# When the halves of the sine tiles are compared: beside the cosine's, or behind the cosine's five rows of tiles

## The chip, the core and the metric

The kernel runs on one NeuronCore of a Trainium2 chip. The metric is device time in microseconds. Five engines have instruction streams of their own, in order: TensorE (PE in the profile; its weight loads PEld), VectorE (DVE), ScalarE (ACT), GpSimd (POOL) and SyncE (SP). The last two issue the transfers from HBM here; SP's queue is in order, so a load that waits for its buffer holds every load behind it. A line number like L387 is a line of the kernel.

## What is computed

```python
h  = x + (Cr @ (xn @ Dr.T) - Ci @ (xn @ Di.T))   # xn = layernorm(x); x is 2048 x 576
r  = layernorm(h) @ w_r                          # one score per token
t  = argmax(r)                                   # a single token
y  = (silu(xs @ w_gate) * (xs @ w_up)) @ w_down  # xs: its normalized row; 4608 hidden columns
out = h + layernorm(h),  and y * sigmoid(r[t]) added to row t
```

`Cr`, `Ci` (2048 x 2048) and `Dr`, `Di` (576 x 576) are the cosine and sine matrices of a Fourier transform, given as inputs in float32.

## The kernel before

**Using and checking the symmetry.** The four matrices are inputs, so the kernel may not assume what is in them. It computes the transform with folded operands (the cosine and sine of an angle give those of its mirror images) and, beside it, compares the parts of the matrices that it uses with those that it doesn't. Each compare writes differences as bfloat16 into a buffer `Q`, ScalarE squares and sums a part of `Q` into one column of `DS`, and at the end a sum over the threshold sends the program into a general path that is not taken here. So all of the matrices is loaded, though only a part of it is multiplied.

**Tiles of the sequence matrices.** A tile (j, i) holds 9 x 128 columns on 128 partitions, 576 KB; i is 0 for the cosine and 1 for the sine. Group one is the rows j = 1 to 5, group two 6, 7, 0 and 8. The tiles that PE multiplies lie in slots of `D`: five slots D0 for the cosine of group one, five D1 for its sine, four D2 (later the cosine of group two). Seven slots `R` and freed slots of `D` form a ring through which all others pass: the mirrored part of a tile (a gather that POOL issues, L301) and the tile of the mirror row 16 - j (SP, L357).

**The checks.** `c_check(j, i)` makes three compares on VectorE: `off_s` for j, `off_s` for 16 - j (L375 each, 896 columns) and `off_t` between the two tiles (L380, 1152 columns). They fill one of the two parts of `Q`, and one square follows (L368, 2944 columns). A ring slot is free for its next load when its last compare has run. There are five checks for the cosine of group one and five for its sine; "check 3" below is that of row 3. `off_h` compares the left half of a tile with the mirrored right half (L387), two instructions for one or two tiles; these are called *halves* here. They read tiles that stay in place for PE, and free no ring slot. In `c_half` the halves of a cosine pair and of the sine pair of the same rows go into one part of `Q`, with one square for both (2304 columns; 1152 for the single fifth row).

**PE's work.** `seq` multiplies the folded tokens by the tiles of a group, in five steps of which 0, 1 and 4 need the cosine tiles and 4, 2 and 3 the sine tiles; `keep` brings each result into a block of `Z` (ScalarE L579, then VectorE L583, called *Z block* here); `hid` multiplies `Z` by the hidden matrices (L610). Then VectorE adds the residual (L619), scores the tokens, picks one, and the weights of its feed-forward part stream through the same buffers (SP L1173), with products on VectorE and POOL and the last product on PE (L1228).

**What sets the order.** The kernel holds a planner: every step is entered with `add`, an estimated duration and what it depends on; `Plan.order` lays out all engines in time, taking on each engine, of the steps that are ready, the one with the longest way to the end, and the instructions are then written out in that order. A buffer is assigned when a step is entered, so the order of the calls from L948 to L999 sets which slot of the ring and which part of `Q` a check gets (`qs.take`, two parts in turn), and with the part which square it waits for:

```python
    for c, m in HALVES[0]:
        c_half(0, c, m)
    for j in GROUPS[0][:3]:
        c_check(j, 0)
    w_first()
    for j in GROUPS[0][3:]:
        c_check(j, 0)
    for n in (0, 1, 4, 2, 3):
        seq_step(0, n)
        keep_step(0, n)
```

Of the kernel before, what the change touches and what calls it, by code (L numbers as in the profile page):

```python
# [14 lines left out]
P = 128  # L15
# [22 lines left out]
GROUPS = [[1, 2, 3, 4, 5], [6, 7, 0, 8]]  # L38
# [5 lines left out]
HALVES = [[(0, 2), (2, 2), (4, 1)], [(0, 2), (2, 2)]]  # L44
# [8 lines left out]
HM = P // 2  # L53
# [17 lines left out]
class Plan:  # L71
# [6 lines left out]
    def add(self, eng, dur, fn, *deps, tail=0.0, push=0.0):  # L78
        flat = []
        for d in deps:  # L80
            flat += d if isinstance(d, list) else [d]
        n = {"eng": eng, "dur": dur, "fn": fn, "deps": [d for d in flat if d], "tail": tail, "push": push}
        n["i"] = len(self.ops)
        self.ops.append(n)
        return n
# [57 lines left out]
def kernel(  # L143
# [172 lines left out]
    Q = QT.bitcast(BF16).rearrange("p (n w) -> p n w", n=2)  # L316
# [62 lines left out]
        o = Q[:, u % 2, 14 * P : QW].rearrange("p (k m) -> p k m", m=P)  # L379
        dve.tensor_tensor(o, C[NK - j, i, False], C[j, i, False][:, :, ::-1], op=SIGN[i])  # L380

    def off_h(g, c, n, i, u):

        o = Q[:, u % 2, i * 9 * n * HM : (i + 1) * 9 * n * HM].rearrange("p (c k m) -> p c k m", k=9, m=HM)
        t = DT[g, i][:, c : c + n]
        for k, op in enumerate((OP.subtract, OP.add)):
            dve.tensor_tensor(o[:, :, k::2, :], t[:, :, k::2, 0:HM], t[:, :, k::2, HM:P], op=op)  # L387
# [296 lines left out]
    add = plan.add  # L684

    def then(f, *args):
        return lambda: f(*args)
# [25 lines left out]
    for k, n in X_LOADS:  # L713
        d = in_turn("SP" if k < 9 else "POOL", then(load_x, k, n), 0.295 * n)
# [11 lines left out]
    for a, b in X_RUNS:  # L726
# [4 lines left out]
        m = [add("ACT", 0.95, then(measure, k), f, push=push) for k, f in zip(ks, r)]  # L731
# [70 lines left out]
    CU = {}  # L802
# [11 lines left out]
            LAST["SP"], d = load("SP", then(load_c, None, j, i, False), 0.59, w, LAST["SP"])  # L814
            CU[j, i, False] = u, d

    def c_half(g, c, m):
        u, w = qs.take()
        cus = [[CU[j, i, False] for j in GROUPS[g][c : c + m]] for i in range(2)]
        n = [  # L820
            add("DVE", 0.16 + 0.62 * m, then(off_h, g, c, m, i, u), [d for _, d in cus[i]], w)
            for i in range(2)
        ]
        for i in range(2):
            for b, _ in cus[i]:
                users[b].append(n[i])
        squares(u, 9 * m * P, n)

    def squares(u, w, n, ps=P):
        SQUARES.append(add("ACT", 0.3 + w / 1200, then(square, u, w, ps), n))  # L830
        qs.users[u].append(SQUARES[-1])

    def c_check(j, i):

        u, w = qs.take()
        u0, d0 = CU[j, i, False]
        c_load(j, i, True)
        u1, d1 = CU[j, i, True]
        n = [add("DVE", 1.08, then(off_s, j, i, u, 0), d0, d1, w)]
        users[u0] += n  # L840
        users[u1] += n
        free.append(u1)
        if j in PAIRS:
            m = NK - j
            c_load(m, i, False)
            c_load(m, i, True)
            (u2, d2), (u3, d3) = CU[m, i, False], CU[m, i, True]
            n.append(add("DVE", 1.08, then(off_s, m, i, u, 1), d2, d3, w))
            users[u3].append(n[1])
            n.append(add("DVE", 1.36, then(off_t, j, i, u), d0, d2, w))  # L850
            users[u0].append(n[2])
            users[u2] += n[1:]
            free.extend([u3, u2])
        if u0[0] == "D1":
            free.append(u0)
        squares(u, QW if j in PAIRS else 7 * P, n)
# [94 lines left out]
        for b in [b for b in free if type(b) is tuple and b[0] == tag]:  # L951
            free.remove(b)

    for c, m in HALVES[0]:
        c_half(0, c, m)
    for j in GROUPS[0][:3]:
        c_check(j, 0)
    w_first()
    for j in GROUPS[0][3:]:
        c_check(j, 0)  # L960
    for n in (0, 1, 4, 2, 3):
        seq_step(0, n)
        keep_step(0, n)
# [18 lines left out]
    for i in range(2):  # L982
        for j in GROUPS[1]:
            c_check(j, i)
    for c, m in HALVES[1]:
        c_half(1, c, m)
    for c in range(2):
        hid_step(0, c)
    for n in (0, 1):
# [514 lines left out]
```

## Time and profile before

| | |
|---|---|
| time, median of 3 runs | 200.77 us (200.58 to 201.01) |
| the profiled execution | 201.27 us, span 199.2 us |
| VectorE busy | 166.1 us (83%), 419 instructions |
| ScalarE busy | 140.5 us (71%), 259 instructions |
| TensorE busy | 130.4 us (65%) |
| GpSimd busy | 122.8 us (62%) |
| moved by DMA | 77.81 MB, 391 GB/s over the span |

A busy row reads: engine, busy time, share of the span, number of instructions. The rows in tenths cut the span into 40 slices of 5 us. A row of a window gives, after its length, the busy time and number of instructions of PE, PEld, DVE, ACT and POOL, the granted clock, the mean busy share of the 16 DMA engines, and GB/s. A row of waits reads: engine, line, what ended the wait, us in total, times, longest. A row in order of time gives the start, the time to the end of the last of its instructions, engine, line, operation, tiles and count, and in brackets the idle time before it and what ended that. "SPq" is SP's queue; the duration of its rows is that of the issue, not of the transfer. Where the releaser named in a wait had long been done, the wait was for something else, often a transfer.

### The profile page before, as it was taken

To read this page: it belongs to the slowest core of one execution; us is meant where nothing else is said; L and a number is where in the kernel's file an instruction comes from. 1 tells how busy PE (TensorE), PEld (TensorE's weight loads), DVE (VectorE), ACT (ScalarE), POOL (GpSimd) and SP (SyncE) were. 2 spreads that over 40 slices of the span, in tenths; PEclk is the share of its full clock that TensorE was granted. 3 is DMA by queue.
4 is the path that set the end of the run, shared out by engine and by line. 5 is a ranking of instruction groups with operands and counts; after the bars stand their busy time and mean duration, and the time that the engine had idled before them with its cause. 6 is when DMAs were issued, how large, how long until landed. Compare 5 with 4: busy or idle time off the path is not lost. (4 is left out here: it accounts for less than half of the span.)

```text
span 199.2 us, 2787 instructions
## 1 busy us (share of the span) xinstructions
PE 130.4 (65%) x758; PEld 89.9 (45%) x758; DVE 166.1 (83%) x419; ACT 140.5 (71%) x259; POOL 122.8 (62%) x134
## 2 busy tenths in 40 slices
PE   0007989999999989899999996600241444085840
PEld 0005667764767778677877774400121111043220
DVE  4389997989999859997999999999839997899410
ACT  2298863783987794799587599997629999786400
POOL 6578888495528878998870000006439999998500
PEclk9999999999999999999999999985555555555798
DMA  5999999999979999999999999999999999999991
GB/s 190 361 418 415 411 411 409 409 372 346 402 275 366 415 398 391 404 407 412 407 401 418 420 420 422 427 414 423 422 428 425 428 422 420 431 420 412 422 387 42
DMA packets 14491, 77.81 MB, mean 391 GB/s; under 512 B 1855, under 2 KB 1859, under 8 KB 11143
## 3 DMA queue, kind: packets, MB, share of 16 engines
q1 hardware_dynamic: 10463, 56.56, 70.8%
q0 software_dynamic: 4000, 21.03, 26.3%
q8 instruction: 7, 0.11, 0.2%
q14 instruction: 13, 0.11, 0.1%
q10 hardware_dynamic: 8, 0.00, 0.0%
HBM read 72.86 MB, written 6.49 MB: 398 GB/s over the span
## 5 line engine op out<-in xcount | busy, mean ns | idle before, releaser
L368 ACT ACTIVATE Q<-Q 128x2944 bf16<-128x2944 bf16 (+5 forms) x26 | 55.4, 2133 | 19.9 <-DVE Q L375 7.0
L610 PE MATMUL py<-W,Z 128*128 128x289 f32 x180 | 45.3, 408 | 2.3 <-DVE X L619 2.3
L565 PE MATMUL ps<-D,XF 128*128 128x320 f32 (+3 forms) x216 | 45.0, 408 | 1.2 <-DMA D<-in_ct_dram 0.8
L301 POOL DMA_INDIRECT R<-in_ct_dram,ic x21 | 34.1, 1625 | 14.5 <-DVE Q L375 10.5
L610 PEld LDWEIGHTS py<-W,Z 128*128 128x128 f32 x180 | 33.7, 189 | 13.6 <-issue 2.9
L565 PEld LDWEIGHTS ps<-D,XF 128*128 128x128 f32 (+1 forms) x216 | 32.1, 172 | 13.8 <-issue 2.5
L1201 POOL TENSOR_TENSOR D<-D,Z 128x1152 f32<-128x1152 f32 x8 | 20.8, 2618 | 1.2 <-SPq L1331 1.2
L667 POOL DMA_DIRECT2D out_dram<-X x1 | 0.6, 606 | 30.0 <-ACT X L661 30.0
L301 POOL DMA_INDIRECT D<-in_ct_dram,ic x11 | 16.1, 1468 | 3.4 <-issue 2.4
L498 ACT ACTIVATE junk<-X,XT 128x576 bf16<-128x576 f32 x16 | 12.4, 772 | 8.0 <-DVE W L459 6.5
L1206 ACT ACTIVATE junk<-D 128x576 bf16<-128x576 f32 x20 | 13.7, 683 | 4.0 <-POOLq L1331 2.3
L1228 PE MATMUL pd<-XF,H 128*1 128x144 f32 x80 | 5.3, 440 | 16.1 <-DVE H L1220 13.3
L537 PE MATMUL fo<-W,diag 128*128 128x288 f32 (+1 forms) x8 | 3.9, 665 | 16.4 <-DVE diag L528 16.4
L387 DVE TENSOR_TENSOR Q<-D 128x640 bf16<-128x640 f32 (+3 forms) x20 | 12.7, 691 | 1.4 <-DMA D<-in_ct_dram 1.4
L380 DVE TENSOR_TENSOR Q<-R,D 128x1152 bf16<-128x1152 f32 x10 | 13.4, 1349 | 0.0
L630 ACT ACTIVATE junk<-X,TD 128x576 bf16<-128x576 f32 x16 | 12.3, 768 | 1.5 <-DVE X L619 1.3
L375 DVE TENSOR_TENSOR Q<-R,D 128x896 bf16<-128x896 f32 x11 | 11.9, 1083 | 1.3 <-DMA D<-in_ct_dram 1.2
L661 ACT ACTIVATE X<-X,BB,UP 128x576 f32<-128x576 f32 x14 | 10.8, 855 | 2.4 <-DVE BB L642 2.4
L623 DVE SCALAR_TENSOR_TENSOR junk<-X,wr 128x576 bf16<-128x576 f32 x16 | 12.1, 754 | 0.3
L375 DVE TENSOR_TENSOR Q<-D 128x896 bf16<-128x896 f32 x11 | 11.8, 1081 | 0.0
L619 DVE SCALAR_TENSOR_TENSOR X<-py,X 128x576 f32<-128x576 f32 x16 | 11.5, 748 | 0.0
L375 DVE TENSOR_TENSOR Q<-R 128x896 bf16<-128x896 f32 x10 | 10.8, 1084 | 0.7 <-DMA R<-in_ct_dram,ic 0.7
(202 smaller groups left out, 262.5 us busy)
## 6 DMA issues: line engine op xcount, KB each, us to landing
D<-in_ct_dram SPq DMA_DIRECT2D x22, 576.0 KB
R<-in_ct_dram SPq DMA_DIRECT2D x10, 576.0 KB
D<-in_wu_dram SPq DMA_DIRECT2D x5, 1152.0 KB
D<-in_wd_dram SPq DMA_DIRECT2D x4, 1152.0 KB
R<-in_wg_dram SPq DMA_DIRECT2D x3, 1152.0 KB
D<-in_wg_dram SPq DMA_DIRECT2D x3, 1152.0 KB
out_dram<-X SPq DMA_DIRECT2D x2, 1440.0 KB
X<-in_x_dram SPq DMA_DIRECT2D x4, 576.0 KB
```

Source lines behind the costliest of these rows:

```text
L301: pool.indirect_dma_start(tile, None, view, bass.IndirectOffsetOnAxis(ap=rows, axis=0), element_offset=at)
L368: act.activation(t, t, AF.Square, accum_out=DS[0 : t.shape[0], n : n + 1])
L375: dve.tensor_tensor(o, C[j, i, True][:, 0:7, :], C[j, i, False][:, 7:0:-1, :], op=SIGN[i])
L380: dve.tensor_tensor(o, C[NK - j, i, False], C[j, i, False][:, :, ::-1], op=SIGN[i])
L387: dve.tensor_tensor(o[:, :, k::2, :], t[:, :, k::2, 0:HM], t[:, :, k::2, HM:P], op=op)
L498: act.activation(junk[:, 0:D], X[:, k, 0:D], AF.Square, bias=XT[:, n : n + 1], scale=-float(D), accum_out=VX[:, n : n + 1],)
L565: pe.matmul(cm(ZP[g, n][k % 2][p0 : p0 + m], w), XF[:, q, m0 : m0 + m], DT[g, i][:, :, k, 0:HM], start=k in (0, 1), stop=k in (6, 7),)
L610: pe.matmul(YP[GROUPS[g][c]][:, h, 0:w], Z[:, a, c * P : (c + 1) * P], w_block(a)[:, h * HD : h * HD + w], start=(a == 0), stop=(a == 4),)
L623: dve.scalar_tensor_tensor(junk2, X[:, k, 0:D], 1.0, wr, op0=OP.mult, op1=OP.mult, accum_out=TD[:, n, 0:1])
L630: act.activation(junk[:, 0:D], X[:, k, 0:D], AF.Square, bias=TD[:, n, 1:2], scale=-float(D), accum_out=VAR[:, n : n + 1],)
L1201: pool.tensor_tensor(t, t, xs.unsqueeze(1).to_broadcast([P, JW, D]), op=OP.mult)
L1206: act.activation(junk[:, 0:D], WB[w, j][:, r, :], AF.Copy, accum_out=acc[:, j + r : j + r + 1])
```

## The change

`off_h` is given the place in its part of `Q`. A new function `halves` takes a list of pairs and a list of matrices (0 for the cosine, 1 for the sine), and puts all their halves behind each other into one part of `Q`, with one square. For group one it is called with the cosine's three pieces ahead of the cosine's checks (one part, one square of 2880 columns), and with the sine's three pieces after the fifth cosine check (a part of its own, one square of 2880 columns). For group two the pieces and squares are as before.

```diff
-    def off_h(g, c, n, i, u):
-
-        o = Q[:, u % 2, i * 9 * n * HM : (i + 1) * 9 * n * HM].rearrange("p (c k m) -> p c k m", k=9, m=HM)
+    def off_h(g, c, n, i, u, at):
+
+        o = Q[:, u % 2, at : at + 9 * n * HM].rearrange("p (c k m) -> p c k m", k=9, m=HM)
...
-    def c_half(g, c, m):
+    def halves(g, parts, ms):
         u, w = qs.take()
-        cus = [[CU[j, i, False] for j in GROUPS[g][c : c + m]] for i in range(2)]
-        n = [
-            add("DVE", 0.16 + 0.62 * m, then(off_h, g, c, m, i, u), [d for _, d in cus[i]], w)
-            for i in range(2)
-        ]
-        for i in range(2):
-            for b, _ in cus[i]:
-                users[b].append(n[i])
-        squares(u, 9 * m * P, n)
+        n, at = [], 0
+        for i in ms:
+            for c, m in parts:
+                cus = [CU[j, i, False] for j in GROUPS[g][c : c + m]]
+                o = add("DVE", 0.16 + 0.62 * m, then(off_h, g, c, m, i, u, at), [d for _, d in cus], w)
+                for b, _ in cus:
+                    users[b].append(o)
+                n.append(o)
+                at += 9 * m * HM
+        squares(u, at, n)
...
-    for c, m in HALVES[0]:
-        c_half(0, c, m)
+    halves(0, HALVES[0], [0])
     for j in GROUPS[0][:3]:
         c_check(j, 0)
     w_first()
     for j in GROUPS[0][3:]:
         c_check(j, 0)
+    halves(0, HALVES[0], [1])
...
-    for c, m in HALVES[1]:
-        c_half(1, c, m)
+    for part in HALVES[1]:
+        halves(1, [part], [0, 1])
```

On VectorE this is how the rows stand behind the last fold (L548), first before. The brackets name the counters that a row waits for: DMAHW those of SP's loads, DMASW those of POOL's gathers.

```order
L548 TENSOR_SCALAR XF<-fo_370 128x287 [waits Activation_49]
L387 TENSOR_TENSOR Q<-D 128x2x5x64 [waits DMAHW7_49]
L387 TENSOR_TENSOR Q<-D 128x2x4x64
L387 TENSOR_TENSOR Q<-D 128x2x5x64 [waits DMAHW4_49,DMAHW3_49]
L387 TENSOR_TENSOR Q<-D 128x2x4x64
L375 TENSOR_TENSOR Q<-R,D 128x896 [waits DMASW4_49,Activation_49]
L375 TENSOR_TENSOR Q<-R 128x896 [waits DMAHW0_49,DMASW5_49,DVE_49]
L380 TENSOR_TENSOR Q<-R,D 128x1152
L387 TENSOR_TENSOR Q<-D 128x5x64 [waits DMAHW2_49,Activation_49]
L387 TENSOR_TENSOR Q<-D 128x4x64 [waits DVE_49]
L387 TENSOR_TENSOR Q<-D 128x5x64 [waits DMAHW7_49]
L387 TENSOR_TENSOR Q<-D 128x4x64
```

And at the same place now, with the first Z block (L583) at the end:

```order
L548 TENSOR_SCALAR XF<-fo_370 128x287 [waits Activation_49]
L375 TENSOR_TENSOR Q<-R,D 128x896 [waits DMASW4_49]
L387 TENSOR_TENSOR Q<-D 128x5x64 [waits DMAHW2_49]
L387 TENSOR_TENSOR Q<-D 128x4x64
L375 TENSOR_TENSOR Q<-R 128x896 [waits DMAHW0_49,DMASW5_49]
L380 TENSOR_TENSOR Q<-R,D 128x1152
L724 TENSOR_SCALAR bt<-tf 128x16
L375 TENSOR_TENSOR Q<-R,D 128x896 [waits DMASW6_49,Activation_49]
L380 TENSOR_TENSOR Q<-R,D 128x1152 [waits DMAHW1_49,DVE_49]
L375 TENSOR_TENSOR Q<-R 128x896 [waits DMASW7_49]
L583 SCALAR_TENSOR_TENSOR Z<-ps_0_0_389,os_0_427 128x5x64 [waits Activation_49]
```

The first compare of check 1 follows the fold directly, and check 2 stands ahead of the first Z block; before, that Z block and the crossed compare (L380) of check 3 stood ahead of check 2.

The second place is the end of the cosine's checks on VectorE, before: the last three rows of check 5's compares, the third and fourth Z block to be written, and the first sine check.

```order
L375 TENSOR_TENSOR Q<-R,D 128x896 [waits DMASW4_49,Activation_49]
L375 TENSOR_TENSOR Q<-R 128x896 [waits DMAHW0_49,DMASW5_49,DVE_49]
L380 TENSOR_TENSOR Q<-R,D 128x1152
L583 SCALAR_TENSOR_TENSOR Z<-ps_2_0_467,os_2_501 128x5x64 [waits Activation_49]
L583 SCALAR_TENSOR_TENSOR Z<-ps_2_0_467,os_2_501 128x5x64
L583 SCALAR_TENSOR_TENSOR Z<-ps_3_0_489,os_3_521 128x5x64 [waits Activation_49]
L583 SCALAR_TENSOR_TENSOR Z<-ps_3_0_489,os_3_521 128x5x64
L375 TENSOR_TENSOR Q<-R,D 128x896 [waits DMASW6_49,DVE_49]
```

And now, from the second compare of check 5 to the last Z block:

```order
L380 TENSOR_TENSOR Q<-R,D 128x1152 [waits DMAHW0_49]
L375 TENSOR_TENSOR Q<-R 128x896 [waits DMASW5_49,DVE_49]
L583 SCALAR_TENSOR_TENSOR Z<-ps_2_0_464,os_2_501 128x5x64 [waits Activation_49]
L583 SCALAR_TENSOR_TENSOR Z<-ps_2_0_464,os_2_501 128x5x64
L387 TENSOR_TENSOR Q<-D 128x2x5x64 [waits DMAHW4_49,DMAHW3_49,DVE_49]
L387 TENSOR_TENSOR Q<-D 128x2x4x64
L387 TENSOR_TENSOR Q<-D 128x2x5x64 [waits DMAHW6_49,DMAHW5_49]
L387 TENSOR_TENSOR Q<-D 128x2x4x64
L583 SCALAR_TENSOR_TENSOR Z<-ps_3_0_490,os_3_520 128x5x64 [waits Activation_49]
L583 SCALAR_TENSOR_TENSOR Z<-ps_3_0_490,os_3_520 128x5x64
L387 TENSOR_TENSOR Q<-D 128x5x64
L387 TENSOR_TENSOR Q<-D 128x4x64
```

The two pairs of sine halves now stand ahead of the last Z block, and the fifth row's behind it, ahead of the first sine check; the first compare of check 5 has moved ahead of the Z block of step 4. Up to the first sine checks VectorE and ScalarE are the only engines whose order differs: PE, SP and POOL issue the same instructions in the same order.

## The prediction

> **What bounds the kernel now.** I read the page first, then the busy time by microseconds where a slice fell off, then what SyncE's queue waited for there, and last the order of time on VectorE, which it waited for. The page:
>
> ```profile
> span 199.2 us, 2787 instructions
> PE 130.4 (65%) x758; PEld 89.9 (45%) x758; DVE 166.1 (83%) x419; ACT 140.5 (71%) x259; POOL 122.8 (62%) x134
> DMA  5999999999979999999999999999999999999991
> GB/s 190 361 418 415 411 411 409 409 372 346 402 275 366 415 398 391 404 407 412 407 401 418 420 420 422 427 414 423 422 428 425 428 422 420 431 420 412 422 387 42
> ```
>
> No engine is full, but the DMA row is: all slices but the first, one in the middle and the last are at nine tenths or more. 77.81 MB have to move, and the program ends when the last weights have come, so a microsecond in which the DMA engines stand dry is added at the end. One slice is at 7 (275 GB/s, 55 to 60 us). By microseconds:
>
> ```profile
> 55.00:56.00 1.00, 1.00 (x5) 0.73 (x4) 1.00 (x1) 0.46 (x4) 0.00 (x0) 1.00 1.01 400
> 56.00:57.00 1.00, 1.00 (x5) 0.68 (x5) 1.00 (x2) 0.79 (x1) 0.00 (x0) 1.00 0.89 363
> 57.00:58.00 1.00, 1.00 (x6) 0.68 (x5) 1.00 (x2) 1.00 (x1) 0.00 (x0) 1.00 0.22 86
> 58.00:59.00 1.00, 1.00 (x5) 0.50 (x4) 1.00 (x2) 1.00 (x3) 0.61 (x1) 1.00 0.87 205
> 59.00:60.00 1.00, 1.00 (x5) 0.56 (x4) 1.00 (x3) 0.80 (x2) 1.00 (x1) 1.00 0.95 341
> ```
>
> The last two columns are the DMA share and GB/s. Against 400 GB/s these rows lack 37, 314, 195 and 59 GB/s from 56 to 60 us: 605/400 = 1.5 us of transfer. (The 346 at 45 to 50 us is something else: the share there is full, the rate low.) What held the loads back, from the waits of SyncE's queue between 40 and 61 us and its issues:
>
> ```profile
> SPq L357 <- DVE Q L375: 11.6, 2, 7.1
> SPq L357 <- DMA R<-in_ct_dram,ic: 3.3, 1, 3.3
> 41.47 0.33 SPq L357 DMA_DIRECT2D R<-in_ct_dram  x1
> 48.98 0.33 SPq L357 DMA_DIRECT2D R<-in_ct_dram  x1
> 57.14 0.33 SPq L357 DMA_DIRECT2D R<-in_ct_dram  x1
> 57.52 0.51 SPq L357 DMA_DIRECT2D D<-in_ct_dram  x1
> ```
>
> SP issued three ring tiles in 16 us, each held by VectorE compares that free the slot. Behind the third stand D loads that go out at once when it has gone: they were ready, and the queue is in order. The compare that ended that wait is the first of the fifth cosine check:
>
> ```profile
> 30.57 1.42 DVE L387 TENSOR_TENSOR Q<-D 128x640 bf16<-128x640 f32 x2
> 33.71 1.43 DVE L387 TENSOR_TENSOR Q<-D 128x640 bf16<-128x640 f32 x2 [1.36 <-DMA D<-in_ct_dram]
> 35.42 2.75 DVE L387 TENSOR_TENSOR Q<-D 128x640 bf16<-128x640 f32 x4
> 38.09 1.08 DVE L375 TENSOR_TENSOR Q<-R,D 128x896 bf16<-128x896 f32 x1
> 39.09 1.08 DVE L375 TENSOR_TENSOR Q<-R 128x896 bf16<-128x896 f32 x1
> 40.10 1.35 DVE L380 TENSOR_TENSOR Q<-R,D 128x1152 bf16<-128x1152 f32 x1
> 41.37 1.56 DVE L387 TENSOR_TENSOR Q<-D 128x320 bf16<-128x320 f32 x4
> 47.87 1.08 DVE L375 TENSOR_TENSOR Q<-R 128x896 bf16<-128x896 f32 x1
> 52.84 1.00 DVE L583 SCALAR_TENSOR_TENSOR Z<-ps,sgn,os 128x320 f32<-128x320 f32 x2
> 56.03 1.09 DVE L375 TENSOR_TENSOR Q<-R,D 128x896 bf16<-128x896 f32 x1
> 60.90 1.08 DVE L375 TENSOR_TENSOR Q<-R,D 128x896 bf16<-128x896 f32 x1
> ```
>
> VectorE has almost no gap here, so only its order can free slots sooner. The halves (L387) of all ten tiles stand ahead of or between the cosine checks, and free nothing that is waited for.
>
> **The change, part by part.** It moves the halves of five sine tiles behind the last cosine check: two pairs of 1.42 us and one of 0.78 (half of 1.56), 3.6 us. Nothing is added on VectorE, and SP, POOL and PE keep their order. ScalarE squares 2 x 2880 columns in place of 2304, 2304 and 1152, one instruction fewer.
>
> ```profile
> 35.17 2.12 ACT L368 ACTIVATE Q<-Q 128x2304 bf16<-128x2304 bf16 x1 [1.23 <-DVE Q L387]
> 37.20 0.18 ACT L368 ACTIVATION_READ_ACCUMULATOR Q<-Q 128x1 f32 x1
> 44.20 1.15 ACT L368 ACTIVATE Q<-Q 128x1152 bf16<-128x1152 bf16 x1
> ```
>
> From 2.12 and 1.15 us, 1152 columns cost 0.97 and an instruction 0.18, so the saving is 0.18 + 0.18 = 0.36 us. ScalarE is idle before most squares, waiting for VectorE, so it is worth nothing.
>
> *The cosine checks, walked on VectorE.* The first pair starts at 30.57 as before and the second cosine pair needs no sine tile, so the wait of 1.36 at 33.71 goes. With two folds between, of the 0.3 to 0.4 that 35.42 stands behind the end of the row before it, and 0.3 allowed for a wait of the second, check 1's first compare starts at 34.4, and the odd tile's halves (0.78) end at 36.2. The next compare reads the direct ring tile that before was read at 39.09 without a wait: when it lands no row tells. The wait is 0 to 2.9 us; I take 1.5, the middle, since the queue was just delivering the sine tiles ahead of it (the row at 33.71 waited for one). Check 1 then ends at 37.7 + 1.0 + 1.3 = 40.0 (41.37 before, which SP waited for), check 2 at 43.4 (48.87 before), Z block, check 3 at 47.5, Z block, check 4 at 51.6 (in steps of 3.3 a check and 0.8 a Z block). Its first compare of check 5 needs a gather: SP's own wait of 3.3 for one ended 4.5 us (11.6 less 7.1) before 57.14, at 52.6. So that compare runs 52.6 to 53.6, and SP issues at 53.7 in place of 57.14. With the wait at 2.9 it is 54 to 55, with none still 53.7. All lie before the DMA ran dry at 56.7: one ring tile and the D tiles, together 3 MB, arrive in the queue in time. That is the gain: **1.5 us**; below it, nothing if the refill is late, and no more than 1.5 from this hole.
>
> *Where the halves go.* From 53.7: Z block 0.9, the rest of check 5 2.3, Z block 0.8, four halves 2.7, Z block 0.8, the last halves 0.75: 62.0 for the first sine compare, against 60.90, so 1.1 us late (0.4 early to 2.6 late with the bounds above). SP's next ring tiles, which wait for the sine checks, go out that much later:
>
> ```profile
> 64.28 0.33 SPq L357 DMA_DIRECT2D R<-in_ct_dram  x1
> R<-in_ct_dram SPq DMA_DIRECT2D x10, 576.0 KB
> 58.39 1.82 POOL L301 DMA_INDIRECT R<-in_ct_dram,ic  x1 [4.25 <-DVE Q L375]
> 61.75 5.58 POOL L301 DMA_INDIRECT D<-in_wt_dram,iw  x1 [0.30 <-issue]
> 67.20 1.09 DVE L375 TENSOR_TENSOR Q<-R 128x896 bf16<-128x896 f32 x1 [0.68 <-DMA R<-in_ct_dram,ic]
> 74.85 0.76 DVE L422 TENSOR_TENSOR Q<-D,W 128x576 bf16<-128x576 f32 x1 [2.38 <-ACT Q L368]
> ```
>
> Cover: SP's six tiles from 53.7 on are 6 x 576 KB, 8.8 us at 400 GB/s, and POOL's gathers come beside them (its 5.58 us instruction reads as one held by a full queue). They reach past 65. The lateness is then paid by two waits of VectorE, 0.68 at 67.20 and 2.38 at 74.85: both are for gathers (the ScalarE square named at 74.85 was long done) that stand behind POOL's wait of 4.25, which ends at the end of check 5's compares, 57 in place of 58.1. So VectorE is level or ahead by 75 us, and every later release with it. If that cover fails, up to 1.1 us comes back.
>
> *The end.* Does the weight stage take 1.5 us of earlier data?
>
> ```profile
> 184.59 2.62 POOL L1201 TENSOR_TENSOR D<-D,Z 128x1152 f32<-128x1152 f32 x1 [1.25 <-SPq L1331]
> 192.24 1.16 PE L1228 MATMUL pd<-W,H 128*1 128x144 f32 x32 [0.94 <-SPq L1331]
> ```
>
> POOL's last product waited 1.25 us and PE's last rows 0.94, with the queue named long done: for weights. POOL then ends at 185.95 even if its start hasn't moved, some 6 us before PE's last rows; it takes the whole gain.
>
> *Sum.* The profiled execution took 201.27 us (span 199.2 and 2.1 around it): 201.27 - 1.5 = 199.8. The median of the runs is 0.5 lower, so **199.3 us**.
>
> **Rivals.**
>
> *Given back later (20%).* The hole closes, but the DMA, 1.5 us ahead, finds VectorE not ahead where its queue is thin again. SP's longest wait after 58 us is for VectorE:
>
> ```profile
> SPq L357 <- DVE Q L375: 17.5, 7, 5.8
> 84.85 0.33 SPq L357 DMA_DIRECT2D R<-in_ct_dram  x1
> 91.75 0.33 SPq L357 DMA_DIRECT2D R<-in_ct_dram  x1
> ```
>
> Seven microseconds without an SP issue were just covered before. If VectorE reaches that compare at the old time, the same 1.5 us is lost there, less what is queued: 0.4 to 0.6 us stays, 200.3. For it: VectorE is late at 62. Against it: the 3.1 us of waits that it can drop before.
>
> *Slower: the halves' lateness opens a larger hole (15%).* Place: the first sine checks. The landing waits add up (the ring tile at 36.2, the tile of check 4 that SP issued last before its stop, the gather at 52.6). If VectorE is late at the first sine compare by more than the 3.1 us of waits that it can drop, releases lag, and SP's tiles of 64.28 and after start that much late with the DMA 1.5 us ahead of them. It decides from 64 us on for that compare; at 66.5 (5.6 late) the DMA lacks 2.5 us in place of the 1.5 saved: 200.77 + 1.0 = 201.8. Against it: my bounds end at 63.5. The Trainium skill's page "DMA: Bandwidth & Descriptors", section "Queues, rings and completion order", speaks for this rival: each DMA engine takes turns between the queues that have work, a packet at a time, so that gathers which POOL issues sooner would take their turns from SP's tiles, and those would land later than before. By the rows the sum is 199.3; by that rule pushed to its end, every tile late, it is this rival's 201.8; no run here shows the split yet.
>
> *The change doesn't do it (10%).* The DMA still runs dry near 57, since some other gather or tile than the slot's compare comes last: 200.7. For it: the wait that ended at 57.14 was for a gather in 3.3 of its 7.8 us. Against it: the gather was in at 52.6.
>
> **How the numbers follow.** My forecast has 55%, with its own range of 198.7 to 200.0 (VectorE's dropped waits may also fill thin places after 75, up to 0.6 more). A measurement of this kernel tells 0.2%, 0.4 us, from no change: faster is under 200.4, slower over 201.2. Faster: 55 and half of the given-back case, 65%. Same: the other half of it and the case without effect, 20%. Slower 15%. The range of 8 in 10 is 198.5 to 201.1.
>
> **What would show it.** Right: no microsecond from 54 to 62 with a DMA share under 0.9; SP's third ring tile issued near 53.7; the first compares of checks 2 and 5 near 40 and 52.6; the first sine compare near 62; the wait of 2.38 at 75 smaller; the last PE rows 1.5 us earlier. Wrong: a dry microsecond that has moved to 64 to 76 or 88 to 93, VectorE idle before a compare of check 1 or 4 for over 3 us, or the same hole at 57.

## The result: 1.3% slower, and the profile after

The changed kernel takes 203.63 us (median of 5, 203.04 to 203.86) against 200.94 us (5 runs, 200.58 to 201.18): 1.0128 of the time before, 95% interval 1.0107 to 1.0149, so 2.7 us more. The prediction said 199.3 us, with 201.1 as its upper bound. The profiled execution took 203.04 us, with a span of 201.1.

The table below gives the median and range of all executions; its ratios leave out executions more than 1.5% above the fastest of their kernel, there is no ratio where a single one is left, and the traces of e1, e2, e4, e10 and e16 are of executions that are left out in this way.

The page of the changed kernel, its busy share of the DMA engines and the rate in slices of 5 us:

```profile
span 201.1 us, 2790 instructions
DMA  5999999999929999999999999999999999999991
GB/s 186 377 419 412 411 411 409 409 396 361 380 71 402 418 381 405 405 409 407 415 405 417 416 425 422 424 423 414 424 429 428 419 427 424 425 421 419 414 380 37
```

The slice that stood at 275 GB/s stands at 71: the hole has grown. By microseconds (columns as in the prediction: after the length PE, PEld, DVE, ACT, POOL, the granted clock, the DMA share, GB/s):

```profile
55.00:56.00 1.00, 0.00 (x0) 0.00 (x0) 0.94 (x1) 0.00 (x0) 0.00 (x0) 1.00 0.48 194
56.00:57.00 1.00, 0.00 (x0) 0.00 (x0) 1.00 (x2) 0.00 (x0) 0.00 (x0) 1.00 0.07 28
57.00:58.00 1.00, 0.00 (x0) 0.00 (x0) 1.00 (x2) 0.48 (x1) 0.31 (x1) 1.00 0.01 5
58.00:59.00 1.00, 0.00 (x0) 0.00 (x0) 1.00 (x3) 1.00 (x1) 1.00 (x1) 1.00 0.00 0
59.00:60.00 1.00, 0.60 (x1) 0.50 (x2) 1.00 (x2) 1.00 (x1) 0.24 (x1) 0.68 0.64 115
60.00:61.00 1.00, 1.00 (x3) 0.67 (x2) 1.00 (x2) 0.87 (x6) 0.00 (x0) 0.50 0.99 332
61.00:62.00 1.00, 1.00 (x3) 0.64 (x2) 1.00 (x3) 0.30 (x1) 0.12 (x1) 0.50 1.01 410
62.00:63.00 1.00, 1.00 (x3) 0.57 (x3) 1.00 (x3) 1.00 (x1) 0.83 (x1) 0.62 1.00 408
```

Against 400 GB/s the first five rows lack 206, 372, 395, 400 and 285: 1658/400 = 4.1 us, where before it was 1.5. The difference, 2.6 us, is about the loss of 2.7. Beside it stands something new: TensorE has nothing to do for five microseconds, and its granted clock is 0.50 to 0.62 for three more when it starts again.

What came before the hole, in order of time on SyncE's queue, GpSimd and VectorE, in the kernel before:

```profile
35.11 0.34 SPq L357 DMA_DIRECT2D D<-in_ct_dram  x1
39.45 4.29 POOL L301 DMA_INDIRECT R<-in_ct_dram,ic  x1 [2.39 <-DVE Q L375]
44.04 0.94 POOL L301 DMA_INDIRECT R<-in_ct_dram,ic  x1 [0.30 <-DVE bt L724]
46.95 1.81 POOL L301 DMA_INDIRECT R<-in_ct_dram,ic  x1 [1.97 <-DVE Q L375]
49.22 0.94 POOL L301 DMA_INDIRECT R<-in_ct_dram,ic  x1 [0.46 <-DVE Q L375]
51.83 1.09 DVE L375 TENSOR_TENSOR Q<-R,D 128x896 bf16<-128x896 f32 x1
```

The first row issues the tile of row 12 (cosine), which SyncE sends out last ahead of its ring tiles; it goes into a `D2` slot. The last row is the first compare that reads it. VectorE did not stand for it by more than 0.2 us. The same in the changed kernel:

```profile
34.37 1.08 DVE L375 TENSOR_TENSOR Q<-R,D 128x896 bf16<-128x896 f32 x1
34.74 0.34 SPq L357 DMA_DIRECT2D D<-in_ct_dram  x1
36.59 1.52 POOL L301 DMA_INDIRECT R<-in_ct_dram,ic  x1 [0.32 <-issue]
38.42 0.96 POOL L301 DMA_INDIRECT R<-in_ct_dram,ic  x1 [0.30 <-issue]
40.32 1.82 POOL L301 DMA_INDIRECT R<-in_ct_dram,ic  x1 [0.94 <-DVE Q L375]
42.59 0.95 POOL L301 DMA_INDIRECT R<-in_ct_dram,ic  x1 [0.45 <-DVE Q L375]
45.66 1.55 POOL L301 DMA_INDIRECT R<-in_ct_dram,ic  x1 [2.12 <-DMA R<-in_ct_dram,ic]
47.10 1.08 DVE L375 TENSOR_TENSOR Q<-D 128x896 bf16<-128x896 f32 x1
55.06 1.36 DVE L380 TENSOR_TENSOR Q<-D 128x1152 bf16<-128x1152 f32 x1 [6.87 <-DMA D<-in_ct_dram]
56.34 2.09 DVE L375 TENSOR_TENSOR Q<-R,D 128x896 bf16<-128x896 f32 x2
58.45 0.33 SPq L357 DMA_DIRECT2D R<-in_ct_dram  x1
67.19 1.08 DVE L375 TENSOR_TENSOR Q<-R,D 128x896 bf16<-128x896 f32 x1
```

Check 1 starts at 34.4 and check 4 at 47.1, as walked. Then VectorE, ready at 48.19, stands for 6.87 us ahead of the crossed compare of check 4. The tile of row 12, issued 0.4 us sooner than before, is in at 55.06 and not by 51.8. The compare that SyncE's third ring tile needs, the first of check 5, stands behind (second of the two at 56.34); the ring tile goes out at 58.45, later than before (57.14). In between GpSimd's gathers had gone out 2.9 to 6.6 us sooner than before. What the two kinds of queue moved between 40 and 48 us (packets, MB, share of the 16 engines; q1 has SyncE's loads, q0 GpSimd's gathers), first before:

```profile
q1 hardware_dynamic: 842, 2.19, 85.4%
q0 software_dynamic: 108, 0.54, 17.3%
```

and in the changed kernel:

```profile
q0 software_dynamic: 380, 2.16, 67.6%
q1 hardware_dynamic: 468, 1.04, 34.8%
```

SyncE's queue got 1.15 MB less in these 8 us, which is 2.9 us at 400 GB/s, and the tile of row 12 is read 3.2 us later (55.06 and 51.83).

### The profile page after: what moved, and what is told of

It reads as the page before. It is cut to its first block, busy times and chain, and to the rows that moved or that the text cites. A ratio compares the mean times of both kernels' runs of the same rounds, so it can differ in the third digit from the quotient of the medians.

```text
span 201.1 us, 2790 instructions
## 1 busy us (share of the span) xinstructions
PE 132.0 (66%) x758; PEld 91.4 (45%) x758; DVE 166.5 (83%) x419; ACT 140.2 (70%) x257; POOL 113.0 (56%) x134
## 5 line engine op out<-in xcount | busy, mean ns | idle before, releaser
L565 PE MATMUL ps<-D,XF 128*128 128x320 f32 (+3 forms) x216 | 46.6, 416 | 5.2 <-DVE Z L583 5.2
L610 PE MATMUL py<-W,Z 128*128 128x289 f32 x180 | 44.8, 408 | 0.5 <-DVE X L619 0.5
L301 POOL DMA_INDIRECT R<-in_ct_dram,ic x21 | 30.2, 1438 | 22.7 <-DVE Q L375 16.6
L565 PEld LDWEIGHTS ps<-D,XF 128*128 128x128 f32 (+1 forms) x216 | 33.1, 177 | 18.1 <-DVE Z L583 5.7
L301 POOL DMA_INDIRECT D<-in_ct_dram,ic x11 | 13.1, 1194 | 5.5 <-DVE Q L380 2.5
L380 DVE TENSOR_TENSOR Q<-R,D 128x1152 bf16<-128x1152 f32 x10 | 13.4, 1350 | 0.0
L380 DVE TENSOR_TENSOR Q<-D 128x1152 bf16<-128x1152 f32 x4 | 5.4, 1350 | 6.9 <-DMA D<-in_ct_dram 6.9
```

Source lines behind the costliest of these rows:

```text
L301: pool.indirect_dma_start(tile, None, view, bass.IndirectOffsetOnAxis(ap=rows, axis=0), element_offset=at)
L565: pe.matmul(cm(ZP[g, n][k % 2][p0 : p0 + m], w), XF[:, q, m0 : m0 + m], DT[g, i][:, :, k, 0:HM], start=k in (0, 1), stop=k in (6, 7),)
L610: pe.matmul(YP[GROUPS[g][c]][:, h, 0:w], Z[:, a, c * P : (c + 1) * P], w_block(a)[:, h * HD : h * HD + w], start=(a == 0), stop=(a == 4),)
```

## The experiments

Three theories were put against each other. **A**: gathers that are released sooner take turns from SyncE's queue, the tile of row 12 comes late, and VectorE, in order, stands with all that would free slots behind it. **B**: that tile's landing is what it is; only VectorE's order makes the stand. **C**: the 3.6 us of halves behind the cosine checks make VectorE late for the sine checks (the prediction's slower rival). A and B can each be half right.

| kernel | us, median (range) | ratio to before (95%) | tile of row 12 read at |
|---|---|---|---|
| the change, again | 203.54 (202.30 to 204.10) | 1.010 (1.006 to 1.014) | 56.0 |
| e14: gathers held from the 2nd | 208.21 (one) | | 51.6 |
| e13: held from the 3rd | 208.16 (one) | | 52.5 |
| e2: held from the 4th | 207.41 (203.69 to 207.57) | | 54.0 |
| e9: 3.7 us added on VectorE | 205.19 (205.05 to 205.39) | 1.021 (1.018 to 1.023) | 54.9 |
| e4: new parts, sine halves early | 207.25 (203.48 to 208.13) | | 50.9 |
| e8: sine halves after check 3 | 210.95 (210.13 to 212.47) | 1.051 (1.045 to 1.056) | 54.7 |
| e3: no sine halves | 203.57 (202.56 to 205.74) | 1.010 (1.008 to 1.013) | 56.1 |
| e1: check 5 first | 202.91 (200.43 to 203.79) | 1.005 (1.001 to 1.009) | 55.4 |
| e18: e1 again | 203.70 (202.88 to 204.33) | 1.011 (1.008 to 1.015) | 55.9 |
| e16: e1 with TensorE kept busy | 201.37 (200.06 to 203.49) | 1.000 (0.998 to 1.002) | 56.1 |
| e17: the change with TensorE kept busy | 206.78 (205.50 to 207.43) | 1.029 (1.027 to 1.031) | 55.4 |
| e15: e1 without sine halves | 201.08 (199.49 to 202.09) | 0.998 (0.995 to 1.000) | 54.7 |
| e5: W tiles behind row 12 | 200.70 (199.81 to 200.96) | 0.999 (0.997 to 1.001) | no wait |
| e10: W tiles behind rows 12 and 11 | 204.40 (200.25 to 205.55) | | no wait |
| e6, e11: as e5 and e10, on the kernel before | 200.93, 201.15 | 0.999 (0.997 to 1.002), 0.997 (0.993 to 1.001) | |
| e7: check 5 first, on the kernel before | 200.97 (200.39 to 201.66) | 1.000 (0.999 to 1.002) | no wait |

**Why the tile is late: gathers held.** One copy of a single element that reads the tile of row 12 keeps GpSimd from issuing the gather behind it.

```diff
         if mirror:
+            if (j, i) == (1, 1):       # e2; (11, 0) in e13, (5, 0) in e14
+                pool.tensor_copy(held, C[12, 0, False][:, 8, P - 1 : P])
             gather(
```

> The change, with GpSimd held, ahead of the gather for the first sine check (row 1), until the tile of row 12 has landed (a one-element copy that reads it). Two gathers of 0.46 MB each then come behind that tile in place of beside it. Theory A: the tile lands 2 us sooner, 52.5 to 53.5 in place of 55.06, SyncE's third ring tile goes out near 56 in place of 58.45, the hole is 1 to 2.5 us in place of 4.3, 200.3 to 202.0 us. Theory B: the tile lands at 55 as in the change, and with the gathers later still the time is 203.6 or more.

> The change with GpSimd held ahead of its third gather (row 11, cosine) until the tile of row 12 has landed, as in the run that held it ahead of the fourth. One gather less, 0.46 MB or 1.15 us at 400 GB/s, lies beside SyncE's queue. Theory A (sharing): the tile lands 1 us or more before that run's 53.95, at 52.3 to 53.2. A landing that does not depend on the gathers: 54 to 56. The time is not what it is for: later than 205 us, since three gathers come behind the tile.

> The change with GpSimd held ahead of its second gather (row 5, cosine) until the tile of row 12 has landed: only one gather is left beside SyncE's queue. Theory A: the tile lands another 1 us or more sooner, at 50.5 to 52.2, as early as in the kernel before or earlier. A landing that does not depend on the gathers: 54 to 56. The time: later than 206 us.

The copy runs when the tile is in. In order of time on GpSimd, with three gathers beside the tile (e2):

```profile
53.99 0.19 POOL L354 COPY held<-D 128x1 f32<-128x1 f32 x1 [11.40 <-DMA D<-in_ct_dram]
```

with two (e13), and with one (e14):

```profile
52.53 0.18 POOL L354 COPY held<-D 128x1 f32<-128x1 f32 x1 [11.34 <-DMA D<-in_ct_dram]
```

```profile
51.63 0.19 POOL L354 COPY held<-D 128x1 f32<-128x1 f32 x1 [11.47 <-DMA D<-in_ct_dram]
```

From SyncE's issue (35.74 in the repeated change, 35.28, 35.30, 35.44) the tile took 20.3 us with all five gathers, 18.7 with three, 17.2 with two and 16.2 with one: 0.8 to 1.5 us for each gather, about its own 0.46 MB at 400 GB/s (1.15 us). These are single traces, but the three runs form a row: the landing is set by the gathers beside it, as A has it, and B falls for the landing. The tile of e2 came half a microsecond behind the expected 52.5 to 53.5, those of e13 and e14 as expected. The time of these kernels is no better than the change's, and mostly worse (e2's fastest is 203.69); the held gathers then come later than in the change, which we take for the reason, though no run shows it apart. So e2 missed its expected 200.3 to 202.0.

**Delay in place of the halves (e9).** Five sums into a scratch tile, 3.7 us, ahead of check 1.

```diff
     for n in plan_ffn(best[1])[1]:
+        if n is CHK[1, 0][0]:
+            for k in range(5):
+                dve.tensor_tensor(junk2, X[:, 0, :], X[:, 0, :], op=OP.add)
         if n["fn"]:
```

> The change with 3.7 us of useless work added on VectorE ahead of the first compare of check 1 (five sums of 576 columns into a scratch tile), and nothing else moved. Theory A (the checks release GpSimd's gathers too soon, and these delay the tile of row 12): the first compare of check 1 starts near 38 as before the change, the gathers go out some 3.5 us later, the tile lands at 51.5 to 53, VectorE waits under 2 us for it, the hole is under 2.5 us, and the time is 200.6 to 202.4 us: more work, and sooner done than the change. Theory B (only the order of VectorE's rows matters): the order is that of the change, and with the work 203.5 or more. Theory C (VectorE late behind the cosine checks): 3.7 us later still, 205 to 207 us.

A's numbers were missed, and the 205.19 us lie where B (203.5 or more) and C (205 to 207) had them. Check 1 started at 38.42, but in order of time on VectorE:

```profile
54.87 1.36 DVE L380 TENSOR_TENSOR Q<-D 128x1152 bf16<-128x1152 f32 x1 [2.64 <-DMA D<-in_ct_dram]
```

The gathers went out at 39.8, 41.5, 44.4, 46.6 and 49.7: the first as late as before, each of the next three still some 2.5 us sooner than before (44.0, 47.0, 49.2), since there check 1 and check 2 lay further apart, with a gather that took 4.29 us to issue. We read it so: what held the gathers back before was the whole spacing of the checks, and 3.7 us in one place do not give it back; the kernel then paid for the delay as well. By its time alone this run does not decide for A; the held gathers above and the W tiles below do.

**Sine halves moved elsewhere (e4, e8).** These enter the steps at another place (e4: both lists ahead of the checks; e8: the sine list after check 3).

```diff
     halves(0, HALVES[0], [0])
+    halves(0, HALVES[0], [1])          # e4
     for j in GROUPS[0][:3]:
         c_check(j, 0)
+    halves(0, HALVES[0], [1])          # e8
```

> The change with the sine halves ahead of the cosine checks again, but still one part and one square for the cosine halves and one for the sine halves. Theory A: with 7.1 us of halves ahead of check 1 its gathers go out as late as before or later, the tile of row 12 lands at 51 to 52.5, 200.4 to 201.6 us (near before). If the new pairing in the buffer were the cause: 203 or more.

> The change with the sine halves entered after check 3 in place of after check 5; on VectorE they stand ahead of the first compare that reads the tile of row 12. Theories A and B: the gathers are as early as in the change, the tile lands near 55 and SyncE's third ring tile goes out near 58, the halves only fill part of VectorE's wait (6.9 less 3.6, some 3 us left), 203.0 to 203.8 us. Theory C: the halves are out of the way of the sine checks, under 201.5 us.

The landing is as A expects (50.9 with the gathers late, at 40.2, 43.3, 47.4 and 51.4; 54.7 with them early), the times are far off, over all the forecasts for e8, and for e4 on the side of the rival, the new pairing in the buffer (203 or more): the planner lays out everything behind such a step anew, and both traces have further holes past 98 us. So e4 tells nothing on the time of the new parts as such. That they need not cost anything shows in e5 below, which has them and the time of before.

**What the late tile costs: check 5 first (e1), and no sine halves (e3).** In e1 one step is taken forward in the finished order; the rest keeps its place.

```diff
-    for n in plan_ffn(best[1])[1]:
+    todo, c5 = plan_ffn(best[1])[1], CHK[5, 0][0]
+    todo = [n for n in todo if n is not c5]
+    todo.insert(min(k for k, n in enumerate(todo) if n is CHK[4, 0][2]), c5)
+    for n in todo:
```

> The change, with the first compare of check 5 put on VectorE ahead of the two compares of check 4 that read the tile of row 12. Theory A (a late tile: GpSimd's gathers, released sooner, take turns from SyncE's queue, the tile of row 12 lands at 55.1 in place of 51.8, and VectorE stands before its first compare with all that would free slots behind it): the tile still lands near 55, VectorE still waits 4 to 6 us there, but the first compare of check 5 runs near 49 to 50, SyncE's third ring tile and four D tiles go out near 50 to 51, no microsecond from 54 to 61 has a DMA share under 0.9, 199.0 to 200.5 us. Theory B (the tile's landing is what it always was, only VectorE's order matters): the same time. Theory C (the 3.6 us of halves behind the cosine checks make VectorE late for the sine checks): the hole only moves past 62, 202.5 to 203.6.

In order of time on VectorE and by stretches in e1:

```profile
49.80 1.09 DVE L375 TENSOR_TENSOR Q<-R,D 128x896 bf16<-128x896 f32 x1 [1.08 <-ACT Q L368]
55.43 1.36 DVE L380 TENSOR_TENSOR Q<-D 128x1152 bf16<-128x1152 f32 x1 [4.54 <-DMA D<-in_ct_dram]
```

```profile
54.00:62.00 8.00, 3.93 (x9) 2.38 (x8) 6.56 (x9) 4.11 (x7) 1.69 (x2) 0.69 1.03 413
62.00:110.00 48.00, 48.00 (x217) 37.36 (x217) 43.59 (x69) 39.52 (x53) 33.40 (x22) 0.98 0.96 362
```

The hole is gone, as A and B had it: 413 GB/s, where the changed kernel has this:

```profile
54.00:62.00 8.00, 2.84 (x6) 1.82 (x6) 6.94 (x9) 3.65 (x7) 1.67 (x2) 0.83 0.53 187
62.00:110.00 48.00, 48.00 (x220) 37.38 (x221) 45.49 (x74) 39.57 (x52) 32.70 (x22) 0.99 1.02 407
```

But the time came down by half at most (1.005 of before), and not at all when the same kernel ran again (e18, 1.011); 199.0 to 200.5 us were expected. The rate from 62 to 110 us fell to 362 (this execution was one of e1's longer ones, 203.61). So something else is late by then. It is not the moved work alone:

```diff
         c_check(j, 0)
-    halves(0, HALVES[0], [1])
     for n in (0, 1, 4, 2, 3):
```

> The change with the halves of the five sine tiles of group one left out (that part of the symmetry is not compared). 3.6 us of VectorE's work behind the cosine checks and a square are gone. Theories A and B: the tile of row 12 still lands near 55 and the hole of 4.3 us at 55 to 61 is the same, 202.8 to 203.8 us. Theory C: VectorE reaches the sine checks 3.6 us sooner and the loss is gone, under 201.0 us.

e3 came out at A's figure, by stretches with the hole as large as ever:

```profile
54.00:62.00 8.00, 2.27 (x6) 1.33 (x5) 5.93 (x7) 3.36 (x6) 1.55 (x1) 0.82 0.47 166
```

3.6 us less work than the change and no gain: C falls as the cause of the loss as it stands. Whether the halves cost something once the hole is closed is the next question.

**Both at once (e15).**

> The change with the sine halves of group one left out (that part of the symmetry is not compared) and the first compare of check 5 ahead of check 4's two compares of the tile of row 12. Two limits in parallel (loads that VectorE's standing row holds back, and VectorE itself late for the sine checks): the hole at 55 to 60 is closed and VectorE is at its next release (SyncE's ring tile of 64.3 before, 70.6 in the change) by 67 to 68, no hole of over 1 us at 90 to 105, 199.8 to 201.0 us, where either alone gave 202.9 and 203.6. A third limit: 202.5 or more.

By stretches, and VectorE's wait:

```profile
54.00:62.00 8.00, 4.97 (x18) 2.96 (x16) 7.28 (x9) 4.84 (x7) 2.12 (x3) 1.00 1.03 415
62.00:110.00 48.00, 44.78 (x199) 34.98 (x200) 41.81 (x69) 35.75 (x50) 26.52 (x21) 0.98 1.00 388
```

```profile
54.70 1.36 DVE L380 TENSOR_TENSOR Q<-D 128x1152 bf16<-128x1152 f32 x1 [3.57 <-DMA D<-in_ct_dram]
```

With both the loss is gone. The second limit shows in the columns of TensorE: it is busy for all of 62 to 110 us in the change and in e1 (48.00), and not here (44.78), where its clock also stayed at 1.00 past the stand. VectorE too is sooner by then: SyncE's next ring tile goes out at 64.45, where the kernel before has 64.28, the change 70.58 and e1 70.77. Whether the missing halves or the clock did it, e15 alone does not say.

**The second limit (e16, e17, e18).** Behind VectorE's stand TensorE waits for a Z block; it stood 5.2 us in the change, 4.1 in e1. Ten useless matmuls fill that stand.

```diff
     for n in todo:
+        if n is SEQ[0, 3][0]:
+            t = ypair("warm")[0]
+            for k in range(10):
+                pe.matmul(t[:, 0:288], ident, XF[:, 0, 0:288], start=True, stop=True)
```

> The change with the first compare of check 5 ahead, and ten useless matmuls of 288 columns on TensorE where it stands for the Z block (3.7 us by 0.37 each; nothing reads their result). If the half clock is what keeps the time up with the hole closed: the granted clock is 1.00 from 54 to 66, TensorE ends the first group's steps 2 us sooner, no hole of over 1 us at 94 to 104, 200.3 to 201.4 us. If the stand itself (or VectorE's lateness) holds the later loads: 202.0 to 203.6, as without the matmuls.

> The change as it is, with the same ten useless matmuls in TensorE's stand of 5.2 us. The hole of 4 us at 55 to 60 is untouched, so whatever the clock does: 202.8 to 203.8 us. If the clock were the larger part of the loss: under 202.

> The change with the first compare of check 5 ahead, as before, on the same chip as the two with matmuls: 202 to 203.5 us in the median; where its trace shows a half clock after the stand, a hole at 94 to 104 with it.

TensorE in order of time in e18, without the matmuls, and its clock:

```profile
59.21 6.74 PE L565 MATMUL ps<-D,XF 128*128 128x320 f32 x14 [4.38 <-DVE Z L583]
```

```profile
54.00:62.00 8.00, 3.62 (x9) 2.09 (x8) 6.11 (x8) 3.67 (x7) 1.25 (x2) 0.74 1.02 410
```

and in e16, with them:

```profile
53.19 5.01 PE L1335 MATMUL warm<-XF,ident 128*128 128x288 f32 x20
59.48 4.04 PE L565 MATMUL ps<-D,XF 128*128 128x320 f32 x14 [0.19 <-DVE Z L583]
```

```profile
54.00:62.00 8.00, 7.81 (x31) 5.54 (x30) 5.85 (x7) 3.40 (x7) 0.99 (x2) 1.00 1.02 408
```

The ten took 5.0 us (20 records), not 3.7. The same step of TensorE (14 records) takes 4.04 us in place of 6.74, and the median goes from 203.70 (e18, 0.2 above its forecast) to 201.37 us, the level of before, though VectorE waits as long as ever for the tile. That is the time forecast for the half clock as the second limit, but the traces do not bear that cause out. The one of e16, of its longest execution (203.49), has the full clock from 54 to 70 us, and yet the later hole that was to go with the half clock, 1.8 us against 400 GB/s between 100 and 103 us. Its emptiest microsecond:

```profile
101.00:102.00 1.00, 1.00 (x6) 0.90 (x5) 1.00 (x3) 0.70 (x2) 1.00 (x1) 1.00 0.09 36
```

And e5 below runs at half clock for 3.4 us and loses nothing by it (its trace is of a usual execution, 200.60):

```profile
67.00:68.00 1.00, 1.00 (x4) 0.70 (x3) 1.00 (x2) 0.20 (x2) 0.70 (x2) 0.50 0.98 396
```

What the traces of e1, e16 and e18 have in common is VectorE's stand: SyncE's next ring tile goes out at 70.77, 70.13 and 71.45, no sooner than in the change (70.58), and the DMA engines, which no longer lost 4 us at 55, run thin at 94 to 104. That looks like the prediction's rival "given back later", but it is argued and not shown: why the median of e16 comes down with VectorE as late as that, no trace tells. The second limit stays open. In the change as it is (e17) the matmuls do not help, as expected with the hole open; that they make it 3 us slower still, at full clock, was not expected. Its trace has the hole and a thin stretch at 75 to 87 us that the change hasn't, as e9's has; its cause stays open too.

**The W tiles out of the way (e5, e10, e6, e11).** SyncE's queue has 1.4 MB of W tiles (576, 576, 148.5 and 72 KB; the expectations say 1.2), in pieces of 2304 bytes, ahead of the tile of row 12. e5 puts them behind it, e10 also behind the ring tile of row 11.

```diff
-    for j in GROUPS[0][:3]:
+    for j in GROUPS[0][:4]:             # e5; e10: all five, then w_first()
         c_check(j, 0)
     w_first()
-    for j in GROUPS[0][3:]:
+    for j in GROUPS[0][4:]:
         c_check(j, 0)
```

> The change, with SyncE's loads of the three W tiles (1.2 MB in pieces of 2304 bytes) put behind the tile of row 12 in its queue. Theory A: the tile lands some 5 us or more sooner, before 50, VectorE's wait of 6.9 us is gone, SyncE's third ring tile goes out near 50 to 52, the hole at 55 to 61 closes, 198.8 to 200.3 us. Theory B (the tile's landing is not what differs from before): also faster, since the tile is moved, so this run tells only whether that tile is the wait. Theory C (lateness of the halves): 202.5 to 203.6, the hole after 62.

By stretches in e5:

```profile
54.00:62.00 8.00, 8.00 (x32) 5.29 (x30) 4.10 (x6) 2.06 (x3) 1.17 (x2) 1.00 1.02 398
```

The wait for row 12 is gone, the hole is closed (SyncE's third ring tile goes out at 52.46) and TensorE does not stand in it: 2.9 us faster than the change, and no faster than before, where 198.8 to 200.3 were expected. The gathers are as early as in the change (36.6 to 45.7), the sine halves stand behind check 5 and the new pairing is there; so neither the halves' place nor the pairing makes the loss, and the tile of row 12, with what stands behind it, does. One thing is not the same: the planner also put the compares of check 4 in another order. And VectorE still stands, 5.47 us, for the ring tile of row 11; but the compare that releases SyncE's third ring tile is ahead of that stand, and the time is that of before.

> The change with the W tiles one place further back in SyncE's queue than in the run that put them behind the tile of row 12: behind the ring tile of row 11 too, for which VectorE waited 5.5 us there. Theory A: that wait falls under 2 us, check 5 ends near 54 in place of 60, the sine checks start 4 us sooner, and the thin stretch of that run at 69 to 73 (264 to 350 GB/s) and at 93 to 96 shrinks: 199.0 to 200.4 us. If what limits then is elsewhere: 200.5 to 201.0 (as that run).

e10 reached 200.25 once and 203.6 to 205.6 in its other executions; nothing is concluded from it.

> The kernel before, with the W tiles behind the tile of row 12 as in the run beside it. VectorE there waited 0.2 us at most for that tile, and reached the first compare of check 5 at 56.0 with no gap. Theory A and B: nothing is freed sooner, the hole of 1.5 us stays, 200.4 to 201.1 us (same). If the tile's landing had bounded the kernel before as well: 199.5 or less.

> The kernel before with the W tiles behind the tiles of rows 12 and 11. VectorE waited for neither before: the hole at 56 to 60 stays as it comes from VectorE's own order: 200.4 to 201.2 us (same). Were it late tiles there as well: 199.8 or less.

On the kernel before, the W tiles change nothing in the time, as expected: there no compare waited for those tiles.

**The hole of the kernel before (e7).** The edit of e1 on the kernel before, ahead of check 4's last two compares.

> The kernel before, with the first compare of check 5 ahead of the last two compares of check 4 on VectorE. It then runs near 54.0 in place of 56.0, and SyncE's third ring tile and the four D tiles go out near 55.1 in place of 57.1. If the hole of 1.5 us at 56 to 60 comes from that release (as the prediction read it): the hole is under 0.5 us, 199.2 to 200.2 us. If something else has it: 200.6 to 201.1 us.

The compare ran at 55.28, since it also waited 1.04 us for ScalarE to square the part of `Q` that it writes, so the release came only 0.7 us sooner; the hole shrank from 1.5 to some 1.0 us, and the time did not move. It lies at the figure for "something else has it", so this run does not bear out that closing the hole shortens the kernel by as much.

> The changed kernel as it is, beside the others on the same chip: 203.0 to 204.0 us, the first compare that reads the tile of row 12 near 55, a hole of 4 us at 55 to 60.

The repeated change came out at the expected time, with its wait at 7.3 us and the tile read 1 us later than expected.

## Why the prediction was wrong, step by step

**What bounds the kernel: right for the loss, too simple for a gain.** In the change the time follows the hole of the DMA engines: 2.6 us more of it, 2.7 us more of time, and neither is there in e5. But a hole that closes does not come off the time by itself: e1 and e18 closed it and kept half of the loss or all of it, and e7 made the old hole 0.5 us smaller for nothing.

**The walk on VectorE: right to 47 us, wrong at check 4.** First compare of check 1 at 34.37 (34.4 forecast), of check 2 at 38.96 (near 40); the wait for the direct ring tile, put at 1.5 us of 0 to 2.9, did not occur (36.20). The step that failed is "check 4 at 51.6 (in steps of 3.3 a check and 0.8 a Z block)". It gave check 4's tiles no landing time, as if they lay there; the bound of 0 to 2.9 us was put on the first ring tile only. VectorE was ready for check 4's direct tile at 48.19, 3.6 us sooner than it was read before, and the tile came 3.2 us later than that, at 55.06: together the stand of 6.87 us. So the first compare of check 5 ended at 58.4 and not at 53.6, and SyncE's third ring tile went out at 58.45 and not at 53.7.

**"SP, POOL and PE keep their order": true, and too little.** The order stayed, the times did not. Each compare that ran sooner released a gather sooner, and the prediction's sum counted only the release that it wanted (SyncE's third ring tile), not the five gathers that come with it on GpSimd.

**The halves: covered up.** The first sine compare came at 67.19 and not at 62.0, for the wait ahead of them. The two later waits of 0.68 and 2.38 did vanish, as forecast, but e3 shows that the halves cost nothing while the hole stood, and e5 that their place behind the checks need not cost anything without it. Between e1 and e15 the missing halves may have counted; that is part of what stays open.

**"That is the gain: 1.5 us": too large as well.** In the two kernels that closed the hole and came back to the time of before without added work (e5, and e15 with the sine halves left out), it stood at 0.999 (0.997 to 1.001) and 0.998 (0.995 to 1.000) of before: 0.2 to 0.5 us, 1.0 at the most. Their traces show where the rest goes: the rate from 62 to 110 us is 397 GB/s in e5 and 388 in e15 (its longest execution), where the kernel before has 403, by stretches:

```profile
62.00:110.00 48.00, 46.72 (x218) 36.45 (x218) 43.75 (x72) 36.24 (x54) 36.82 (x20) 1.00 1.02 403
```

That is like the rival "given back later", which would have been the nearer forecast if the hole had closed.

**The slower rival (15%): half of the mechanism right, its place and its weight wrong.** It put the loss down to late halves, which were not the cause; but it named landing waits that add up, and the tile of check 4 among them, and it had the gathers' turns from the Trainium skill; it looked for the damage at the first sine checks and priced it at 201.8. The damage was ahead of check 5, at 55 us. Of the Trainium skill's rule (page "DMA: Bandwidth & Descriptors", section "Queues, rings and completion order": an engine takes turns between queues, a packet at a time) the prediction said that no run showed the split yet. The traces agree with it, in packets as the profile counts them (that these are the page's packets no run shows). Between 40 and 44 us of the changed kernel, with gathers and loads queued side by side:

```profile
q0 software_dynamic: 205, 1.13, 71.2%
q1 hardware_dynamic: 203, 0.47, 31.1%
```

In the same four microseconds it is 199 to 200 in e1, 199 to 198 in e2 and 177 to 173 in e5. Over the 8 us shown above it is 380 to 468. The gathers' packets are 5.7 KB on average (2.16 MB by 380) and those of SyncE's queue, with the W tiles in it, 2.2 KB, so turns by packet gave the gathers twice the bytes.

## What to carry to other kernels

When work is taken out from ahead of a chain of releases, walk every transfer that the chain releases, not only the one that is wanted: loads in another queue that were sent long ago can land later because of it. In an engine with one in-order stream, ask of each compare ahead of the critical release whether its data can be the last to land, and put those whose data is in ahead of it. A stand of one engine has more than one price: close the first, and look at what stood beside it.

## What the hardware showed beyond that

In these traces two queues that both have work share the DMA engines by packet and not by byte: 205 packets to 203 in 4 us of the change, but 1.13 MB to 0.47. So small pieces (2304 bytes here) in a load queue lose to gathers of 5.7 KB, and a tile of 576 KB behind them took 20.3 us from issue to use with five gathers beside it, 16.2 with one.

TensorE's granted clock fell to 0.50 in or behind a stand of 5.2 us (change), 4.1 (e1) and 4.4 (e18). It stayed there for 3.4 us (change, e5, e8, e9) or twice that, 6.8 us (e1, e3, e12, e18). The length of the stand does not decide: the clock also fell, up to 1.1 us after work had resumed, behind stands of 2.55 (e8), 2.65 (e9) and 2.97 (e5), and held at 1.00 through 3.03 (e15) and 3.69 (e2). The Trainium skill's page "TensorE: Matmul & The Clock Gate", section "Part 1: The HAM clock gate", has half rate after an idle window of about 3.4 us, with windows that run freely. The traces agree on the 3.4 us, as the length of the slow phase, but not that the engine must be idle for a whole window: three of these stands were shorter. What the slow phase costs off the matmuls' own path is not shown here: e16, with the stand filled, was 2.3 us faster than e18 (201.37 and 203.70), but e5 had it at the time of before.
